# Loads, weight pieces and work units of a fused attention and feed-forward kernel in a new order, with other group sizes

## The chip, the cores and the metric

The kernel runs on one core of one Trainium2 chip. The metric is device time in microseconds (us); lower is better. Engines are called PE (TensorE, matrix multiplies), DVE (VectorE), ACT (ScalarE), POOL (GpSimd) and SP (SyncE, which here only issues DMA transfers). Each works through its own instruction list in order. A "run" is one execution; a median of several runs is quoted. A version was compared with the kernel before on the same chip, in alternating rounds.

## The reference

Linear attention with decay over 4 batches, 8 heads, 768 positions and 64 dimensions, then a feed-forward block (512 to 2048 to 512) with SiLU, all float32 at the boundary:

```python
for b in range(nb):                       # blocks of positions within a head
    intra = einsum('bhic,bhjc->bhij', qb, kb) * Dmask
    intra = einsum('bhij,bhjd->bhid', intra, vb)
    inter = einsum('bhid,bhde->bhie', qb * lam_pow, kv_state)
    out[:, :, sl] = intra + inter
    kv_state = lam_block * kv_state + einsum('bhsd,bhse->bhde', kb * rev_pow, vb)
x = out.transpose(0, 2, 1, 3).reshape(3072, 512)
h = x @ w_in
y = (h * sigmoid(h)) @ w_out
```

## The kernel before

The 3072 tokens are 24 chunks of 128, six to a batch. A chunk's attention has four pieces on PE: `t` (transposes of q and k), `d` (update of the running kv state), `s` (scores) and `o` (output, which ends as columns of `xt`). Chunks are collected into groups. For a group, 16 "up" units (`ffn1`) compute the hidden layer, 128 features each, and "down" units (`ffn2`, a quarter of the sum over features for 128 tokens) the result. The main loop mixes the up units of one group with attention pieces of the next and down units of the one before. Names in the profiles: `tp` are the transposes, `qbd` and `kt` their copies for PE, `sp` the scores and `ss` the masked scores, `kv_ps` and `kvs` the state and its copy, `op` the attention output; `hp` (later `h_ps`) and `o_ps` are the results of up and down units, `g` and `ob` their copies.

```python
GROUPS = [512, 256, 256, 512, 512, 512, 512]
wio = tile_pool(name="wio", bufs=3)      # float32 weight pieces
io  = tile_pool(name="io", bufs=7)       # q, k, v as loaded
opool = tile_pool(name="opool", bufs=3)  # results on their way out
# ... (cut)
def prep(c):
    qf, kf, vf = raw.pop(c)
    nc.gpsimd.tensor_tensor(qb, qf, <lam_fwd>, op=AL.mult)
    nc.gpsimd.tensor_tensor(kb, kf, <lam_bwd>, op=AL.mult)
    nc.scalar.activation(vb, vf, AF.Copy)        # the cast of v is issued here
# ... (cut)
def ffn2(g, mt, kos):
    # ... (cut) four matmuls into o
    if kos[-1] == KO_OUT - 1:
        nc.vector.tensor_copy(ob, o)
        nc.sync.dma_start(out=out[r0:r0 + BLK, :], in_=ob)   # same queue as the loads
# ... (cut) start: load chunks 0 to 3, then w_in; attention of chunks 0 to 3
for m in range(16):                     # up units of group 0
    ffn1(0, m)
    # ... (cut) cast_w("in", 2), cast_w("in", 3), load_w("out", 1..3) on the way
for i in range(4):
    cast_w("out", i)                    # all four casts, on DVE, ahead of chunk 4
while loads and loads[0] < n0 + 6:
    load_c(loads.pop(0))                # chunks 6 to 9 are queued at once
# ... (cut)
for g in range(1, len(GROUPS)):
    while done_c < cst[g] + nch[g]:     # attention pieces that are still missing
        next_att()                      # prepares one chunk ahead, loads one more
        next_down(g)
    npieces = 4 * (nch[g + 1] if g + 1 < len(GROUPS) else 0)
    acc = 0.0
    for m in range(16):
        ffn1(g, m)
        next_down(g)
        acc += npieces / 16.0
        while acc >= 1.0:
            next_att()
            acc -= 1.0
```

## Time and profile before

| | before |
|---|---|
| median of 3 runs | 257.65 us (256.52 to 258.14) |
| span of the profiled run | 254.6 us, mean granted PE clock 0.970 |
| PE busy in the span | 221.1 us |
| first up unit | 24.85 us |
| PE nearly idle | 40.9 to 53.2 us |

The span runs from the first to the last instruction; the device time of the same run was 256.3 us. The first excerpt is the table of stretches of the kernel before, 6 us each. After the stretch and its length it gives, for each engine, busy us and the number of instructions, then the granted clock (1.00 is full), the DMA engines' busy share, and GB/s.

```profile
...
42.00:48.00 6.00, 1.55 (x4) 0.41 (x3) 1.35 (x2) 0.00 (x0) 0.00 (x0) 0.73 1.03 387
48.00:54.00 6.00, 1.16 (x6) 0.59 (x6) 4.30 (x7) 0.00 (x0) 2.08 (x2) 0.50 1.06 235
54.00:60.00 6.00, 5.78 (x28) 3.13 (x28) 2.10 (x4) 2.15 (x5) 2.79 (x3) 0.63 1.30 224
...
```

PE works 1.55 and 1.16 of 6 us in the first two of these stretches, while the DMA engines are busy all the time, and from the second on its clock is down to 0.50 and 0.63. The second excerpt is the timeline of the kernel before: start in us, length in us, engine, line of the program, operation, output from input; in brackets the engine's idle time just before and what ended it.

```profile
...
45.17 1.23 DVE L112 CAST w_out_bf<-t 128x2048 bf16<-128x2048 f32 x1 [9.41 <-DMA t<-in_moe_w_out_dram]
46.45 1.86 PE L235 MATMUL o_ps<-w_out_bf,g 128*128 128x512 bf16 x4 [5.33 <-DVE w_out_bf L112]
...
47.88 1.23 DVE L112 CAST w_out_bf<-t 128x2048 bf16<-128x2048 f32 x1 [1.48 <-DMA t<-in_moe_w_out_dram]
...
50.67 1.23 DVE L112 CAST w_out_bf<-t 128x2048 bf16<-128x2048 f32 x1 [1.57 <-DMA t<-in_moe_w_out_dram]
...
51.81 0.41 DVE L159 COPY qbd_101<-tp 64x512 bf16<-64x512 bf16 x1
...
53.16 1.03 PE L186 MATMUL sp<-qbd_101,kt 128*128 128x256 bf16 x4 [4.84 <-DVE kt L161]
...
```

DVE waits 9.41 us for a piece of `w_out`, the second of four (the first was cast at 34.53), then for two more. Chunk 4's copies (`qbd`, at 51.81) stand behind these casts in DVE's list although their own input, the transposes, was ready at about 40. PE's score piece `sp` waits for them until 53.16. The third excerpt is the list of waits of PE over the whole kernel before: who waited for whom, us in total, how often, the longest.

```profile
...
PE sp L186 <- DVE kt L161: 6.6, 5, 4.8
PE o_ps L235 <- DVE w_out_bf L112: 5.3, 1, 5.3
PE hp L221 <- ACT xt L212: 3.4, 10, 0.4
...
```

The first two are the hole. The third is the first up units of a group, which wait for ACT to copy the last chunk's output to `xt`.

### The profile page before, as it was taken

The page shows a single profiled execution, that of the slowest core. Times are in us where ns is not written, and L with a number is a line of the kernel's source. Part 1 is how long each engine was busy: PE and PEld are TensorE (multiplying, and loading weights), DVE is VectorE, ACT ScalarE, POOL GpSimd, SP SyncE. Part 2 cuts the span into 40 slices and gives each one's busy share as a digit, 9 for nine tenths or more (in the row PEclk, how much of TensorE's full clock was granted, in tenths as well). Part 3 has the DMA queues.
Part 4 walks back from the last instruction along what each step waited for, and adds up shares of the span by engine and source line. Part 5 has one row for each costly group of instructions (what it writes and reads, how often), then busy time and mean ns, then how long its engine had stood idle before and what let it go on. Part 6 is the DMA issues. An engine that isn't in the chain of part 4 may idle for free.

```text
span 254.6 us, 3566 instructions
## 1 busy us (share of the span) xinstructions
PE 221.1 (87%) x1353; PEld 124.9 (49%) x1376; DVE 102.0 (40%) x177; ACT 112.9 (44%) x238; POOL 51.1 (20%) x57
## 2 busy tenths in 40 slices
PE   0756994269998899899998999998999999999994
PEld 0534442035567667555565555554555544444441
DVE  2678410464345457434463534453353430111221
ACT  4146774003428455736585356535535543333000
POOL 3650033063113333331242231132000000000000
PEclk9999999559999999999999999999999999999998
DMA  6999899999999766945397011101101110111122
GB/s 132 220 259 374 290 232 290 337 221 217 195 269 272 164 148 140 221 74 127 84 230 138 0 41 45 41 1 44 41 0 44 41 41 0 44 41 41 41 85 82
DMA packets 82721, 33.79 MB, mean 133 GB/s; under 512 B 75536, under 2 KB 75536, under 8 KB 82704
## 3 DMA queue, kind: packets, MB, share of 16 engines
q1 hardware_dynamic: 82560, 33.56, 56.3%
q8 instruction: 11, 0.18, 0.3%
q14 instruction: 6, 0.05, 0.1%
q10 hardware_dynamic: 144, 0.00, 0.0%
HBM read 27.27 MB, written 6.29 MB: 132 GB/s over the span
## 4 chain that ended last, share of the span: by engine, by line
PE 73%; DVE 7%; DMA 6%; ACT 5%; SPq 5%; issue 2%; POOL 1%
PE o_ps L235 32%; PE hp L221 25%; DMA t<-in_moe_w_out_dram 5%; PE sp L186 4%; PE op L206 3%; PE op L209 3%; PE tp L156 2%; DVE ss L189 2%; SPq L133 2%; ACT xt L212 2%; PE tp L154 2%; ACT xt L211 2%; PE kv_ps L173 2%; SPq L132 1%; DMA lam_sb<-in_lam_dram 1%
## 5 line engine op out<-in xcount | busy, mean ns | idle before, releaser
L221 PE MATMUL hp<-xt,w_in_bf 128*128 128x512 bf16 (+1 forms) x433 | 98.0, 347 | 6.0 <-ACT xt L212 3.4
L235 PE MATMUL o_ps<-w_out_bf,g 128*128 128x512 bf16 x376 | 96.4, 385 | 5.9 <-DVE w_out_bf L112 5.3
L224 ACT ACTIVATE g<-hp 128x512 bf16<-128x512 f32 (+1 forms) x112 | 59.7, 537 | 80.1 <-PE hp L221 78.4
L235 PEld LDWEIGHTS <-g 128*128 128x128 bf16 x384 | 38.0, 99 | 46.9 <-issue 7.1
L221 PEld LDWEIGHTS <-w_in_bf 128*128 128x128 bf16 x448 | 42.4, 98 | 37.0 <-issue 7.7
L142 POOL TENSOR_TENSOR qb<-qf,lam_fwd 128x512 bf16<-128x512 f32 x24 | 25.0, 1044 | 113.8 <-PE tp L154 76.0
L189 DVE TENSOR_TENSOR ss<-sp,mask 128x512 bf16<-128x512 f32 x48 | 31.1, 686 | 21.4 <-PE sp L186 21.2
L239 DVE COPY ob<-o_ps 128x512 f32<-128x512 f32 x24 | 16.6, 692 | 53.0 <-PE o_ps L235 53.0
L211 ACT ACTIVATE xt<-op 64x256 bf16<-64x256 f32 x48 | 18.1, 377 | 31.6 <-PE op L209 29.4
L143 POOL TENSOR_TENSOR kb<-kf,lam_bwd 128x512 bf16<-128x512 f32 x24 | 25.0, 1043 | 12.7 <-PE kv_ps L173 10.5
L206 PE MATMUL op<-ss,vb 128*128 128x256 bf16 x96 | 22.4, 284 | 0.9 <-DVE ss L189 0.6
L144 ACT ACTIVATE vb<-vf 128x512 bf16<-128x512 f32 x24 | 15.0, 625 | 9.1 <-DMA vf<-in_v_dram 9.0
L212 ACT ACTIVATE xt<-op 64x256 bf16<-64x256 f32 x48 | 18.2, 380 | 0.6
L154 PE MATMUL tp<-ident,qb 128*128 128x128 bf16 x96 | 9.7, 227 | 8.3 <-POOL qb L142 6.8
L186 PEld LDWEIGHTS <-kt 128*128 128x128 bf16 x96 | 9.1, 101 | 16.0 <-DVE kt L161 9.6
L176 DVE CAST kvs<-kv_ps 128x512 bf16<-128x512 f32 x20 | 13.7, 687 | 6.2 <-PE kv_ps L173 6.2
L154 PEld LDWEIGHTS <-qb 128*128 128x128 bf16 x96 | 7.6, 101 | 12.9 <-POOL qb L142 6.7
L206 PEld LDWEIGHTS <-vb 128*128 128x128 bf16 x96 | 9.7, 102 | 4.5 <-DVE ss L189 0.9
L159 DVE COPY qbd_99<-tp 64x512 bf16<-64x512 bf16 x8 | 3.3, 416 | 19.7 <-PE tp L156 19.7
L112 DVE CAST w_out_bf<-t 128x2048 bf16<-128x2048 f32 x4 | 4.9, 1227 | 15.4 <-DMA t<-in_moe_w_out_dram 15.4
L186 PE MATMUL sp<-qbd_101,kt 128*128 128x256 bf16 x32 | 5.6, 298 | 5.7 <-DVE kt L161 4.8
L161 DVE COPY kt<-tp 128x512 bf16<-128x512 bf16 x24 | 10.2, 425 | 0.3
(36 smaller groups left out, 98.3 us busy)
## 6 DMA issues: line engine op xcount, KB each, us to landing
qf<-in_q_dram SPq DMA_DIRECT2D x24, 256.0 KB, 4.9
kf<-in_k_dram SPq DMA_DIRECT2D x24, 256.0 KB, 5.0
vf<-in_v_dram SPq DMA_DIRECT2D x24, 256.0 KB, 5.0
out_dram<-ob SPq DMA_DIRECT2D x24, 256.0 KB, 2.0
t<-in_moe_w_in_dram SPq DMA_DIRECT2D x4, 1024.0 KB, 8.5
t<-in_moe_w_out_dram SPq DMA_DIRECT2D x4, 1024.0 KB, 9.0
lam_sb<-in_lam_dram ACTq DMA_DIRECT2D x1, 4.0 KB, 3.0
```

Source lines behind the costliest of these rows:

```text
L142: nc.gpsimd.tensor_tensor(qb, qf, lam_fwd[:, blk, :][:, :, None].to_broadcast([128, H, D]), op=AL.mult)
L143: nc.gpsimd.tensor_tensor(kb, kf, lam_bwd[:, blk, :][:, :, None].to_broadcast([128, H, D]), op=AL.mult)
L154: nc.tensor.transpose(tp[:, 0, p, :], pair_of(qb, p), ident)
L186: nc.tensor.matmul(sp[:, 2 * j:2 * j + 2, :], lhsT=kt[:, p, :], rhs=qt[:, p, :, :], start=True, stop=True)
L189: nc.vector.tensor_tensor(ss, sp, mask[:, None, :].to_broadcast([128, 4, BLK]), op=AL.mult)
L206: nc.tensor.matmul(op[:, j, :, :], lhsT=pair_of(vb, p), rhs=res[half][:, 2 * j:2 * j + 2, :], start=True, stop=(blk == 0))
L211: nc.scalar.activation(xt[g][0:64, 2 * half:2 * half + 2, csl], op[0:64, :, 0, :], AF.Copy)
L212: nc.scalar.activation(xt[g][64:128, 2 * half:2 * half + 2, csl], op[64:128, :, 1, :], AF.Copy)
L221: nc.tensor.matmul(hp[:, :n], lhsT=w_in_bf[:, ko, m * 128:(m + 1) * 128], rhs=xt[g][:, ko, :], start=(ko == 0), stop=(ko == KO_IN - 1))
L224: nc.scalar.activation(gg, hp[:, :n], AF.Silu)
L235: nc.tensor.matmul(o, lhsT=gt[g, ko][:, mt * BLK:(mt + 1) * BLK], rhs=w_out_bf[:, ko, :], start=(ko == 0), stop=(ko == KO_OUT - 1))
L239: nc.vector.tensor_copy(ob, o)
```

## The change

Its intent: PE should always have work for which the data has arrived. The first weight pieces are smaller, and the two chunks of the second group come between weight pieces; the up units of the first group start on half of its tokens; attention of chunks 4 and 5 and some down units are placed among the last up units; the `w_out` casts are spread. Groups are 512, 256, 256, 4 x 384, 512. In later stretches units, pieces and down units are sorted by fractions of the stretch. Some first-group copies go from DVE to ACT, and a table load for SiLU is brought forward. A path with DMA transposes is prepared but never taken (`NPET` is 24). Cut to its core:

```diff
-GROUPS = [512, 256, 256, 512, 512, 512, 512]
+GROUPS = [512, 256, 256, 384, 384, 384, 384, 512]
+NPET = 24
+    for i in range(NQBD):                        # for the path not taken
+        t = const.tile([128, NP, 4, D], BF16, name=f"qpad{i}")
+        nc.gpsimd.memset(t, 0.0)
+    nc.scalar.activation(warm, mask[:, 0:1], AF.Silu)
+    W_IN = [(0, 256), (256, 512), (512, 1024), (1024, 1536), (1536, 2048)]
# prep: the cast of v is put off
-        nc.scalar.activation(vb, vf, AF.Copy)
+        vraw[c] = vf                             # cast in vcast(c), later
# first group: kt and kvs on ACT, half of xt on DVE, transposes in another PSUM tag (another set of buffers for matmul results)
+        if first:
+            nc.scalar.activation(kt, tp[:, 1, :, :], AF.Copy)
# ... (cut) the start, in the order of arrival:
+    for c in range(4):
+        load_c(c)
+    for i in range(5):
+        load_w("in", i)
+        if i == 3:
+            load_c(4)
+    load_c(5)
+    load_w("out", 0)
# ... (cut) attention of chunks 0 to 3
+    ffn1(0, 0, 0), ffn1(0, 1, 0)                 # first half of the tokens
+    st_o(3)
+    ffn1(0, 0, 1), ffn1(0, 1, 1)
# ... (cut) up units 2 to 15 with chunks 4 and 5 among them
+    cast_w("out", 0)
+    st_s(5), st_d(5)
+    ffn2(0, 0, range(0, 4))
+    st_o(5)
+    ffn2(0, 1, range(0, 4))
+    load_c(6)
+    load_c(7)                                    # later loads: one for each prep
# ... (cut)
+    def stretch(*parts):                         # part: items, from, to (fractions)
+        units = []
+        for i, (items, a, z) in enumerate(parts):
+            units += [(a + (z - a) * (j + 0.5) / len(items), i, j, it) for j, it in enumerate(items)]
+        for _, _, _, (fn, *args) in sorted(units, key=lambda u: u[:3]):
+            fn(*args)
# casts: w_out casts 1 to 3; early: the down units of chunks 0 and 1 that use them
+    stretch((ups(1), 0, 1), (casts, 0.0, 0.7), (early, 0.2, 0.9), ([(next_prep,), (next_prep,)], 0.6, 0.8),
+            (downs(0, range(2, 4)), 0.9, 1.3))
+    stretch((downs(1, range(2)), 0, 1), (pieces(2), 0, 0.8))
+    for g in range(2, len(GROUPS)):
+        parts = [(ups(g), 0, 1), (pieces(g + 1), 0, 0.85)]
+        if g > 2:
+            parts.append((downs(g - 1, range(nch[g - 1])), 0, 1))
+        stretch(*parts)
```

## The prediction

> **What bounds the kernel now.** From about 66 us, the tensor engine (PE): the windows table has it busy 8.6 to 9.95 of each 10 us, and the waits list from 66 us gives it 4.1 us of waits, 3.4 of them for `xt` at group starts. Before that, arriving data. The timeline shows the first four chunks' loads issued until 14.3 us; first up-projection at 24.85; a `Silu` table load of 1.28 us at 25.3; PE dense to about 40.7. Then it stands almost still until 53.2 (busy 1.55 of 6 us in 42:48, 1.16 in 48:54), because VectorE's queue holds four `w_out` casts ahead of chunk 4's copies: one waited 9.41 us for its DMA (casts at 45.17, 47.88, 50.67). The granted clock is then 0.50 in 48:54, 0.63 in 54:60. The Trainium skill ("TensorE: Matmul & The Clock Gate", What's actually happening) says an idle window of ~3.4 us halves the clock; this trace agrees.
>
> PE's work at full clock, an estimate from trace pitches (four 512-column matmuls 0.86 us; a chunk's attention about 1.95): 82.9 + 82.9 + 24 x 1.95 = 212.6 us. The span is 254.6: 42 us are start, hole, slow clock, small waits and tail.
>
> **What the change does.** PE's operations stay. Removed: the hole and its slow clock (an estimate: 188.6 us of work remained at 53.2). `w_in` comes in smaller first pieces interleaved with chunks 4 and 5, so PE has their attention, 16 units and 2 down pieces to do while `w_out` arrives. The first up units start on half the tokens; the table load goes to the idle start; in the first group some copies move to ScalarE, and transposes take another PSUM tag, so no longer wait for `ss` (0.78 us each). Added: 16 more, shorter `Silu`; three POOL memsets for a path never taken, in its idle start: no cost.
>
> **The critical path after.** Bytes are the same; the DMA view shows chunks at about 220 GB/s, weights at 386, with 1.6 us from last byte to cast. I estimate visible: first `w_in` 21, last 34; chunk 5 37.6; `w_out` 40.3, 43, 45.7, 48.4. PE does units 0 to 11 by 34.3, waits about 2.3 us for the last `w_in` cast and chunk 4's copies queued behind it, 1 to 1.5 at chunk 5 and the first `w_out` cast, and starts group 1 at 47.2 with 27.2 us of work done. Remaining: 185.4 at full clock, 5 of waits (the down-only stretch of group 1 and the 256-token stretch carrying three chunks are tight: VectorE 3.3 of 3.6 us per chunk), 2.9 tail: span 240.5. Times run 1.7 to 3 above span: **242.5 us**, range 235 to 249. Chances: faster 0.96, same 0.03, slower 0.01. Nearly all the gain is before 66 us; the 384-token groups bring 2 us or less.
>
> **What would show it.** Right: no PE wait above 3 us after 25; clock 1.00 from 15 us; first up unit at 21.5 to 22.5, group 1 at 46 to 49; PE busy 9.7 of 10 from 60; `xt` waits below 1.5 us. Wrong: half clock after 40; `hp` waiting over 3 us for `w_in` casts; many `sp` or `op` waits for VectorE in stretches with two or three chunks.
>
> **What would make it wrong.** VectorE, waiting in order for a weight piece, could hold PE until the clock halves (3 to 6 us slower); chunks 8 to 11 could be late in the short 256-token stretch; better DMA overlap could bring 235.

## The result and the profile after

The changed kernel took 243.66 us (median of 4 runs, 243.06 to 244.62), against 257.65 before. The ratio is 0.9466 with a 95% interval of 0.9418 to 0.9515. Ratios here are the mean time of one kernel's fast runs over that of the other's of the same rounds, so they are not quite the ratio of the medians. The profiled run's span is 241.4 us.

| | before | after |
|---|---|---|
| median | 257.65 us | 243.66 us |
| span, granted clock of the profiled run | 254.6, 0.970 | 241.4, 0.997 |
| first up unit | 24.85 us | 24.12 us |
| up unit 2 of group 0 starts | about 27.3 us | 28.05 us |
| first up unit of group 1 | 64.0 us | 47.90 us |

First the same stretches of the changed kernel.

```profile
...
42.00:48.00 6.00, 4.96 (x35) 2.85 (x34) 5.16 (x8) 3.54 (x9) 0.00 (x0) 1.00 1.03 378
48.00:54.00 6.00, 5.83 (x43) 3.99 (x41) 1.94 (x2) 3.25 (x9) 2.32 (x2) 1.00 0.94 207
54.00:60.00 6.00, 6.00 (x42) 4.02 (x41) 1.25 (x2) 2.23 (x7) 3.37 (x4) 1.00 1.16 217
...
```

The hole and the half clock are gone. The DMA engines were nearly as busy as before (378, 207 and 217 GB/s against 387, 235 and 224). Next the timeline of the changed kernel around the arrival of `w_out`.

```profile
...
44.03 1.22 DVE L145 CAST w_out_bf<-w_tmp 128x2048 bf16<-128x2048 f32 x1
...
45.30 1.02 PE L308 MATMUL o_ps<-w_out_bf,g 128*128 128x512 bf16 x4 [0.52 <-DVE w_out_bf L145]
...
46.36 2.35 DVE L145 CAST w_out_bf<-w_tmp 128x2048 bf16<-128x2048 f32 x2
...
47.90 2.40 PE L293 MATMUL h_ps<-xt,w_in_bf 128*128 128x256 bf16 x16
...
50.58 1.23 DVE L145 CAST w_out_bf<-w_tmp 128x2048 bf16<-128x2048 f32 x1 [1.87 <-DMA w_tmp<-in_moe_w_out_dram]
...
51.39 1.32 POOL L174 TENSOR_TENSOR qb<-qf,lam_fwd 128x512 bf16<-128x512 f32 x1 [13.93 <-DMA qf<-in_q_dram]
...
```

The four casts of `w_out` start between 44.0 and 50.6; before, one started at 34.5 and the others between 45.2 and 50.7. The last piece thus comes no earlier, but now PE has attention, up units and early down units in between, and waits 0.52 us for one cast. The last line shows POOL starting on chunk 6's q as it lands, at 51.39, where the kernel before did at 51.82: by then as many bytes have arrived. The list of waits of PE of the changed kernel:

```profile
...
PE sp L248 <- ACT kt L217: 3.2, 3, 1.6
...
PE o_ps L308 <- DVE w_out_bf L145: 0.5, 1, 0.5
PE h_ps L293 <- ACT xt L279: 0.4, 1, 0.4
...
```

What did not improve is the start. The timeline of the changed kernel shows chunk 3 on its way to the first up unit:

```profile
...
16.45 0.42 PE L268 MATMUL op<-ss,vb 128*128 128x256 bf16 x1
...
16.66 0.42 PE L271 MATMUL op<-qbd_101,kvs 128*128 128x256 bf16 x1
...
20.27 0.27 PE L268 MATMUL op<-ss,vb 128*128 128x256 bf16 x1
...
20.37 0.27 PE L271 MATMUL op<-qbd_103,kvs 128*128 128x256 bf16 x1
...
21.43 0.60 ACT L217 ACTIVATE kt<-tp 128x512 bf16<-128x512 bf16 x1 [0.81 <-DVE qbd_99 L215]
...
22.08 0.61 PE L248 MATMUL sp<-qbd_99,kt 128*128 128x256 bf16 x4 [0.78 <-ACT kt L217]
...
22.70 0.63 ACT L143 ACTIVATE w_in_bf<-w_tmp 128x512 bf16<-128x512 f32 x1
...
23.24 0.62 ACT L191 ACTIVATE vb<-vf 128x512 bf16<-128x512 f32 x1
23.90 0.38 PE L232 MATMUL kv_ps<-vb,kb 128*128 128x128 bf16 x4 [1.21 <-ACT vb L191]
...
24.12 1.04 PE L293 MATMUL h_ps<-xt,w_in_bf 128*128 128x256 bf16 x8
...
```

The last six lines are a chain through ACT, which now does the `kt` copy, a weight cast and the v cast one after the other; the first up unit stands behind the kv matmuls at 24.12. Unit 2, which follows all of units 0 and 1, starts at 28.05, later than the 27.3 of the kernel before. So the rearranged first units bring nothing that these traces show; the gain is after 40 us.

The first four lines show the clock by the spacing of matmuls of equal size: 0.21 us apart until 18 us, 0.10 to 0.11 after. That agrees with the Trainium skill ("TensorE: Matmul & The Clock Gate", What's actually happening), which calls the half clock the default until activity releases it. It would explain why four transposes took 0.61 us at first and 0.39 later. When the full clock comes differs from run to run: in the kernel before, matmuls of 256 columns already stand 0.11 us apart at 16.24, and in the experiment without memsets below, whose start is otherwise that of the changed kernel, the score piece at 13.94 takes 0.61 us, where the one at 13.91 here takes 1.03. There unit 2 starts at 27.45, so about 0.6 us of the later start is the clock of this one run.

The changed kernel has two sorts of fast runs: spans of 241.4 us at a mean clock of 0.997 or 0.998, and of 242.5 to 242.9 at 0.993. No trace of the second sort was kept for this kernel. One was for the experiment with 512-token groups and pieces over the whole stretch, which has the same start: its clock is 0.57 in 24 to 28 us, and the first up unit's eight matmuls take 1.83 us in place of 1.04. Differences near 1 us between versions have to be read with that in mind.

### The profile page after: what moved, and what is told of

Same layout as the page of the kernel before. It is cut to its first block, busy times and chain, and to the rows that moved or that the text cites. A ratio compares the mean times of both kernels' runs of the same rounds, so it can differ in the third digit from the quotient of the medians.

```text
span 241.4 us, 3766 instructions
## 1 busy us (share of the span) xinstructions
PE 220.5 (91%) x1448; PEld 131.4 (54%) x1448; DVE 102.1 (42%) x178; ACT 118.3 (49%) x257; POOL 55.2 (23%) x60
## 4 chain that ended last, share of the span: by engine, by line
PE 83%; DVE 7%; ACT 5%; issue 2%; DMA 1%; POOL 1%; ACTq 0%; DVEq 0%
PE o_ps L308 33%; PE h_ps L293 32%; PE op L268 4%; PE op L271 3%; PE sp L248 3%; PE tp L211 2%; PE tp L209 2%; PE kv_ps L232 2%; DVE ss L251 2%; DMA lam_sb<-in_lam_dram 1%; ACT xt L279 1%; DVE kt L219 1%; ACT xt L278 1%; ACT kt L217 1%; ACT vb L191 1%
## 5 line engine op out<-in xcount | busy, mean ns | idle before, releaser
L293 PE MATMUL h_ps<-xt,w_in_bf 128*128 128x384 bf16 (+2 forms) x520 | 99.5, 323 | 1.6 <-ACT g L297 0.8
L297 ACT ACTIVATE g<-h_ps 128x384 bf16<-128x384 f32 (+2 forms) x128 | 62.3, 491 | 76.1 <-PE h_ps L293 75.1
L308 PE MATMUL o_ps<-w_out_bf,g 128*128 128x512 bf16 x384 | 94.9, 379 | 0.5 <-DVE w_out_bf L145 0.5
L293 PEld LDWEIGHTS <-w_in_bf 128*128 128x128 bf16 x520 | 50.0, 98 | 35.1 <-issue 2.8
L278 ACT ACTIVATE xt<-op 64x256 bf16<-64x256 f32 x44 | 16.6, 377 | 18.9 <-PE op L271 9.9
L279 ACT ACTIVATE xt<-op 64x256 bf16<-64x256 f32 x44 | 16.7, 380 | 0.5
L238 DVE CAST kvs<-kv_ps 128x512 bf16<-128x512 f32 x16 | 11.0, 685 | 1.9 <-PE kv_ps L232 1.9
L211 PE MATMUL tp<-ident,kb 128*128 128x128 bf16 x96 | 10.0, 230 | 0.4 <-POOL kb L183 0.4
L271 PEld LDWEIGHTS <-kvs 128*128 128x128 bf16 x80 | 8.0, 100 | 3.9 <-issue 1.3
L232 PE MATMUL kv_ps<-vb,kb 128*128 128x128 bf16 x80 | 8.2, 228 | 1.5 <-ACT vb L191 1.5
L232 PEld LDWEIGHTS <-kb 128*128 128x128 bf16 x80 | 6.5, 102 | 4.5 <-issue 2.2
```

Of the source, the lines that this page charges most:

```text
L232: nc.tensor.matmul(kv[:, p, :], lhsT=pair_of(kb, p), rhs=pair_of(vb, p), start=(blk == 0 and p == 0), stop=True, skip_group_check=True)
L278: nc.scalar.activation(xt[g][0:64, ps, csl], op[0:64, :, 0, :], AF.Copy)
L279: nc.scalar.activation(xt[g][64:128, ps, csl], op[64:128, :, 1, :], AF.Copy)
L293: nc.tensor.matmul(hp[:, a:z], lhsT=w_in_bf[:, ko, m * 128:(m + 1) * 128], rhs=xt[g][:, ko, a:z], start=(ko == 0 and a == 0), stop=(ko == ...
L297: nc.scalar.activation(gg, hp[:, :n], AF.Silu)
L308: nc.tensor.matmul(o, lhsT=gt[g, ko][:, mt * BLK:(mt + 1) * BLK], rhs=w_out_bf[:, ko, :], start=(ko == 0), stop=(ko == KO_OUT - 1))
```

## The experiments

Twelve kernels ran, all with correct results, with five further rounds each. The kernel before had medians of 257.06, 255.88, 255.65 and 256.03 us in the four submissions; versions are best compared within one submission. All came out of one question: which part of the change makes the gain?

### Submission 1 (before: 257.06 us)

**Only the `w_out` casts moved, in the kernel before.** This is the reading of the prediction taken alone: fill the hole by putting three casts and their down units behind the attention of chunks 4 and 5. Chunk 6 and 7's pieces come after group 1's up units.

```diff
-    for i in range(4):
+    for i in range(1):
         cast_w("out", i)
# ... (cut)
+    late = [1, 2, 3]                # cast just ahead of the first down unit that needs it
+        if g == 0:
+            order = [(mt, kk) for kk in range(4) for mt in range(2)] + order[8:]
# ... (cut) next_down:
+            if late and downs[0][2][0] == 4 * late[0]:
+                cast_w("out", late.pop(0))
# ... (cut) main loop:
             next_att()
-            next_down(g)
+            if g > 1:
+                next_down(g)
-        npieces = 4 * (nch[g + 1] if g + 1 < len(GROUPS) else 0)
+        npieces = 4 * (nch[g + 1] if 1 < g < len(GROUPS) - 1 else 0)
```

> The kernel before, with one thing changed: three of the four w_out casts, and the down pieces that use them, come after the attention of chunks 4 and 5, and group 2's attention after group 1's up units. No small weight pieces, no new load order, no engine moves, 512-token groups. Theory A (the gain is the filled hole at 41 to 53 us and its half clock): PE dense from 46 to 48 us, clock 1.00 throughout, 246 to 249 us. Rival B (arrival order, small first weight pieces and half units make the gain): no better than 254.

Measured: 259.04 us (257.99 to 260.36), ratio 1.0084. Theory A failed in this form, and the number alone would have favoured the rival. The timeline of this experiment tells why:

```profile
...
49.45 3.48 DVE L112 CAST w_out_bf<-t 128x2048 bf16<-128x2048 f32 x3
...
55.01 0.63 ACT L144 ACTIVATE vb<-vf 128x512 bf16<-128x512 f32 x1 [8.85 <-DMA vf<-in_v_dram]
55.66 0.38 ACT L211 ACTIVATE xt<-op 64x256 bf16<-64x256 f32 x1
...
56.48 0.58 PE L221 MATMUL hp<-xt,w_in_bf 128*128 128x256 bf16 x2 [5.60 <-ACT xt L212]
...
```

The casts no longer stand in the way, and chunk 5's output was computed by 51. But `prep(6)` had put chunk 6's v cast into ACT's list ahead of chunk 5's `xt` copies; it waited 8.85 us for its DMA, and the up units of group 1 for `xt`, 5.60 us, until 56.48. A second wait of the same kind had been hidden behind the first: in the kernel before that v cast ran only at 58.44, when its data had landed.

**The groups of before, in the changed kernel.**

```diff
-GROUPS = [512, 256, 256, 384, 384, 384, 384, 512]
+GROUPS = [512, 256, 256, 512, 512, 512, 512]
```

> The changed kernel with the groups of before (512-token groups in place of 384). Theory A: the start is the same to 66 us; 0 to 2 us slower, so 243.5 to 245.5. Rival C (the smaller groups carry a good part of the gain): 248 or more.

Measured: 248.58 us (247.90 to 249.79), ratio 0.9679: 4.9 us slower than the changed kernel's 243.66, more than the prediction allowed. The rival's number was met. At equal clock (0.997) the spans are 246.2 and 241.4. The timeline of this experiment shows one of the places:

```profile
...
142.85 0.60 PE L248 MATMUL sp<-qbd,kt 128*128 128x256 bf16 x4
...
143.27 1.29 DVE L251 TENSOR_TENSOR ss<-sp,mask 128x512 bf16<-128x512 f32 x2 [2.23 <-PE sp L248]
...
144.02 0.27 PE L268 MATMUL op<-ss,vb 128*128 128x256 bf16 x1 [0.56 <-DVE ss L251]
...
```

The output piece follows its score piece with nothing between, so PE waits for DVE's masking in full. In the order of instructions this happens four times (0 us of PE work between `s` and `o`), and never in the changed kernel, where that distance is at least 0.43 us of work. With 16 pieces in 0.85 of a stretch and 16 up and 16 down units in all of it, two pieces sometimes fall between the same two units. The four waits add up to 2.3 us. Part of the rest shows in the 256-token stretch: from 66 to 108 us, PE is busy 37.9 us here and 40.0 in the changed kernel (one of the four waits lies in it). Four chunks' attention rather than three is pressed there between the 16 small up units; that this is the reason was not tested by itself.

**The first group's engine moves undone, in the changed kernel.** `kt`, `kvs` and weight casts on DVE, all `xt` copies on ACT, transposes in the `att` buffers.

```diff
-        if first:
-            nc.scalar.activation(kt, tp[:, 1, :, :], AF.Copy)
-        else:
-            nc.vector.tensor_copy(kt, tp[:, 1, :, :])
+        nc.vector.tensor_copy(kt, tp[:, 1, :, :])
# likewise kvs, xt, the first two weight casts and the PSUM tag
```

> The changed kernel with the first group's engine moves undone: kt and kvs copies back on VectorE, all xt copies and no weight cast on ScalarE, transposes back in the att buffers. Theory A: the up units of the first group wait for the last w_in piece (cast at 34.3) in any case, so group 1 starts within 0.7 us of 47.9 and the time is within 1 us of the changed kernel, even if the first up unit shifts by 1 to 2 us. Rival D (the moves shorten the start): 1.5 to 4 us slower.

Measured: 242.53 us (241.68 to 242.74), ratio 0.9429: 1.1 us faster than the changed kernel's two medians (243.66, and 243.65 for the next experiment, which equals it). Part of that is the clock: five of those ten runs are of the 0.993 sort and none of the six here. Among the runs at 0.997 or more the spans are 239.9 to 241.0 here and 241.0 to 241.6 there, 0.8 us apart in the mean. The rival is out: the moves do not shorten the start, they lengthen it a little. But my reason was wrong too. The first up unit starts at 23.19 in place of 24.12, unit 2 at 27.38 in place of 28.05, and the shift is still there at the end; the last `w_in` piece did not absorb it. A reason why moving `kt` to ACT brings nothing is in the Trainium skill ("PSUM — Partial Sum Buffer", PSUM bank collisions raise a hardware error): two engines may not touch one bank and quadrant at once, reads included, so the program has to put one after the other. This trace agrees: in the changed kernel DVE's copies of that bank end at 9.20 and ACT's `kt` copy, which waited for them, starts at 9.30 and takes 0.60 us; on DVE it starts at 9.23 and takes 0.42. No run put the two in different banks.

**Attention pieces to the end of the stretch, in the changed kernel.**

```diff
-        parts = [(ups(g), 0, 1), (pieces(g + 1), 0, 0.85)]
+        parts = [(ups(g), 0, 1), (pieces(g + 1), 0, 1)]
```

> The changed kernel with the attention pieces of the next group spread over the whole stretch (fraction 1 in place of 0.85). Theory A: the waits of the first up unit of each group for xt come back, about 0.4 to 0.5 us for each of six groups, so 2 to 3 us slower (245.5 to 247). Rival E (placement does not matter once PE is dense): within 0.7 us.

Measured: 243.65 us (242.71 to 244.66), ratio 0.9484: no difference. The waits for `xt` do come back, but only 1.1 us of them after 60 us (four waits), and waits for `kt` fall from 0.9 to 0.8 us. So the fraction of 0.85 as such is worth nothing that these runs can show.

### Submission 2 (before: 255.88 us)

**All v casts out of the preparation, on top of the first experiment.** The v cast goes from `prep` to the head of `st_d`.

```diff
-        nc.scalar.activation(vb, vf, AF.Copy)
+        vraw[c] = vf
# ... (cut)
+    def vcast(c):
+        if c in vraw:
+            nc.scalar.activation(natb[c][2], vraw.pop(c), AF.Copy)
# st_d, first lines:
+        qb, kb, vb = natb[c]
+        vcast(c)
```

> The first experiment showed a second block behind the first: ScalarE's cast of v for chunk 6, issued ahead of chunk 5's xt copies, waited for its DMA until 55.0, and the up units of group 1 for xt until 56.5. This kernel is the first experiment with the v casts moved out of the preparation to the kv piece, as the change does. Theory A2 (the hole is two in-order waits, one on VectorE and one on ScalarE, and both have to go): group 1 starts at 50 to 52 in place of 56.5, no wait over 3 us after 45, 251 to 254 us. Rival: another block appears and it stays at 257 or more.

Measured: 264.69 us, ratio 1.0323. Slower still. One of six runs took 478.64 us, and that was the profiled one. Slow runs are not compared, so this profile explains nothing; that the kv matmuls of every chunk then wait for ACT was argued from the order, not shown (the slow profile lists six such waits, 5.7 us in all).

**512-token groups with the pieces over the whole stretch, in the changed kernel.** The two edits of submission 1 together.

```diff
-GROUPS = [512, 256, 256, 384, 384, 384, 384, 512]
+GROUPS = [512, 256, 256, 512, 512, 512, 512]
-        parts = [(ups(g), 0, 1), (pieces(g + 1), 0, 0.85)]
+        parts = [(ups(g), 0, 1), (pieces(g + 1), 0, 1)]
```

> 512-token groups as in the second experiment, with the pieces over the whole stretch, so that no score piece is followed at once by its output piece (four times in that experiment, with 0.64 us of stall each). Theory F (of the 4.9 us that the 384-token groups bring, about 2 come from fractions that fall together in the 512-token stretches, the rest from four chunks in the 256-token stretch): 246 to 247.2 us. Rival (the size itself matters): 248 or more.

Measured: 245.93 us (244.72 to 246.74), ratio 0.9592, against 243.6 for the next kernel, which equals the changed one. So of the 4.9 us, this edit takes back 2.6; at a clock of 0.997 or more the spans are 243.0 to 243.6, against 246.2. The coinciding fractions are gone with it: PE's waits for `ss` after 60 us, 2.3 us in four before, are no longer listed. The remaining 2.3 us belong to the 512-token groups with the stretch that feeds them; this experiment does not divide them further.

**The last `w_in` and first `w_out` piece loaded ahead of chunks 4 and 5, in the changed kernel.**

```diff
     for i in range(5):
         load_w("in", i)
-        if i == 3:
-            load_c(4)
-    load_c(5)
     load_w("out", 0)
+    load_c(4)
+    load_c(5)
```

> The changed kernel with the last w_in piece and the first w_out piece loaded ahead of chunks 4 and 5. Same bytes, so the arrival of the last thing needed is the same. Theory A: the last w_in piece is cast at about 30.5 in place of 34.3, chunk 4 comes about 4 us later than before and PE waits for it instead; group 1 starts within 1 us of 47.9, and the time is within 1 us of the changed kernel. Rival B (the arrival order matters): 2 us or more slower.

Measured: 243.60 us (243.43 to 244.69), ratio 0.9517: the same. The last `w_in` cast starts at 30.46 in place of 34.34, POOL's work on chunk 4's q at 34.17 in place of 27.89, and PE waits for neither. The exact arrival order of these four pieces does not matter; between 28 and 48 us the changed kernel has slack in both.

**A 256-token first group.** Chunks 0 and 1, `w_in`, chunks 2 and 3, `w_out`; groups 256, 256, 4 x 384, 2 x 512; engine moves and memsets out.

```diff
-GROUPS = [512, 256, 256, 384, 384, 384, 384, 512]
+GROUPS = [256, 256, 384, 384, 384, 384, 512, 512]
+    load_c(0), load_c(1)
+    for i in range(4):
+        load_w("in", i)
+    load_c(2), load_c(3)
# ... (cut) attention of chunks 0 and 1; up units 0 to 11 with three w_in casts
+    prep(2)
+    cast_w("in", 3)
# ... (cut) loads of the last w_out piece and of chunks 4 to 6
+    ffn1(0, 12), ffn1(0, 13)
+    st_t(2)
+    ffn1(0, 14), ffn1(0, 15)
+    prep(3)
+    st_s(2), st_d(2)
+    st_t(3), st_o(2), st_s(3), st_d(3), st_o(3)
# stretch of group 1, with all early down units of group 0:
+    stretch((ups(1), 0, 0.45), (casts, 0.0, 0.5), (early, 0.12, 0.6), (downs(1, range(2)), 0.6, 1), (pieces(2), 0.5, 0.95))
# ... (cut) engine moves and memsets taken out as in their own experiments
```

> A new start: first group of 256 tokens, so two chunks, w_in, two chunks, w_out, then the rest; first-group engine moves and unused memsets left out; groups 256, 256, 4 x 384, 2 x 512. Theory G (up to 48 us PE is limited by what has arrived, and weights bring more work per byte than chunks): estimate from 220 and 386 GB/s: last w_in cast at 24.5, last w_out at 42.4, PE dense from 26 to 33 on, 15 to 17 us of idle up to 42 in place of 20.7 up to 47.9; 237 to 240.5 us. Rival (start is bound by the chain of attention, not by arrival): 242 or more.

Measured: 241.68 us (240.94 to 242.51), ratio 0.9428 (0.9385 to 0.9472): the lowest median, 1.9 us below the changed kernel's equal. But it also leaves out the engine moves, and the changed kernel without these had a ratio of 0.9429 in submission 1. By the ratio, then, the smaller first group adds nothing to that; by the distance to the changed kernel's equal (1.9 us here, 1.1 there) it would add 0.8 us. The runs do not settle it; this version beats both kernels, and the removal of the engine moves can account for at least a good part. It is less than theory G expected. The up units of group 0 start at 17.27 in place of 24.12, but most of that is given back, as this excerpt of its timeline shows:

```profile
...
17.27 8.05 PE L283 MATMUL h_ps<-xt,w_in_bf 128*128 128x256 bf16 x56 [0.26 <-DVE w_in_bf L141]
...
29.62 0.40 PE L205 MATMUL tp<-ident,qb 128*128 128x128 bf16 x4 [1.10 <-POOL qb L170]
30.62 0.40 PE L207 MATMUL tp<-ident,kb 128*128 128x128 bf16 x4 [0.60 <-POOL kb L179]
...
35.43 0.38 PE L283 MATMUL h_ps<-xt,w_in_bf 128*128 128x256 bf16 x2 [0.42 <-ACT xt L269]
...
```

Chunk 3 now arrives late (PE waits for POOL's preparation of it at 29.62 and 30.62), its attention is a chain of waits with no other work beside it, and group 1's up units begin at 35.43.

### Submission 3 (before: 255.65 us)

**Only chunk 6's v cast moved, on top of the first experiment.**

```diff
-        nc.scalar.activation(vb, vf, AF.Copy)
+        if c == 6:
+            vraw[c] = vf                # cast at the head of st_d(6)
+        else:
+            nc.scalar.activation(vb, vf, AF.Copy)
```

> The kernel of the first experiment with only chunk 6's v cast moved behind chunk 5's xt copies; all other v casts stay in the preparation (moving all of them to the kv piece let the kv matmuls of every chunk wait for ScalarE, and cost 5 us more). Theory A2 (two in-order waits make the hole: VectorE for w_out, ScalarE for v of chunk 6): group 1 starts at 50 to 52 in place of 56.5, 251 to 254.5 us, no PE wait over 3 us after 20. Rival: 257 or more.

Measured: 259.18 us (256.86 to 259.84), ratio 1.0107. Group 1 starts at 51.27, as theory A2 said, and PE is dense to 75. The time did not fall, and once more the timeline names the next wait:

```profile
...
72.59 1.09 SPq L133 DMA_DIRECT2D vf<-in_v_dram  x1
...
73.78 6.48 SPq L248 DMA_DIRECT2D out_dram<-ob  x4
...
79.20 0.69 DVE L246 COPY ob<-o_ps 128x512 f32<-128x512 f32 x1 [10.87 <-DMA out_dram<-ob]
79.81 0.41 DVE L164 COPY qbd<-tp 64x512 bf16<-64x512 bf16 x1
...
81.15 1.04 PE L193 MATMUL sp<-qbd,kt 128*128 128x256 bf16 x4 [5.96 <-DVE kt L166]
...
```

`SPq` is the queue from which SP issues transfers. The stores of the first results stand in it behind the loads of chunks 6 to 12, which fill it until 73.68. There are three `ob` buffers, so DVE's fourth `ob` copy waits 10.87 us for the first store to land, chunk 6's copies stand behind it in DVE's list, and PE waits 5.96 us. The clock is at half from 79.7 to 86.5 after it.

**The changed kernel without the unused memsets.**

```diff
-    for i in range(NQBD):
-        t = const.tile([128, NP, 4, D], BF16, name=f"qpad{i}")
-        nc.gpsimd.memset(t, 0.0)
-        qpad.append(t)
```

> The changed kernel without the three unused memsets on POOL. The profile of the changed kernel shows VectorE's 128x6 cast at 2.46 taking 2.30 us in place of 0.11 while they run. Expected: that cast is back at about 0.11 us, lam_fwd still starts at 5.2 to 5.4 because ScalarE's table load ends then, and the time is the changed kernel's within 0.7 us.

Measured: 244.25 us (242.50 to 244.98), ratio 0.9543: no difference. DVE's small cast goes back from 2.30 us (first excerpt, changed kernel) to 0.11 (second, this experiment):

```profile
...
2.00 0.95 POOL L86 MEMSET qpad_105<- 128x1024 bf16 x1
...
2.46 2.30 DVE L92 CAST iota_f<-iota_i 128x6 f32<-128x6 int32 x1
...
5.27 0.24 ACT L102 ACTIVATE lam_fwd<-lam_exp 128x48 f32<-128x48 f32 x1
...
```

```profile
...
2.46 0.11 DVE L88 CAST iota_f<-iota_i 128x6 f32<-128x6 int32 x1
...
5.30 0.24 ACT L98 ACTIVATE lam_fwd<-lam_exp 128x48 f32<-128x48 f32 x1
...
```

`lam_fwd` starts at 5.27 and 5.30: ACT's table load ended then in both (3.98 and 4.01, each with 1.28 us). The Trainium skill ("SBUF — State Buffer", Terms) says that DVE and POOL share a port pair under an exclusive lock. The trace agrees that DVE was held while POOL worked, for as long as all three memsets lasted, and no longer without them; that it was by this lock, no run shows.

**Chunks 2 and 3 among the `w_in` pieces, on top of the small first group**, with their attention among the up units and each `w_in` cast split between DVE and ACT.

```diff
-    for i in range(4):
-        load_w("in", i)
-    load_c(2), load_c(3)
+    load_w("in", 0), load_c(2), load_w("in", 1), load_c(3), load_w("in", 2), load_w("in", 3)
# cast_w: every w_in piece, half on each engine
+        if which == "in":
+            nc.vector.tensor_copy(dst[:, 0:2, :], t[:, 0:2, :])
+            nc.scalar.activation(dst[:, 2:4, :], t[:, 2:4, :], AF.Copy)
# ... (cut) t, s, d, o of chunks 2 and 3 between up units 3 and 11
```

> As the small first group, with chunks 2 and 3 loaded between the w_in pieces and their attention between the up units, and each w_in cast split between VectorE and ScalarE. In the small-first-group run chunks 2 and 3 came after w_in, and group 1's up units waited until 35.4 us with 14.7 us of PE work done. Theory G: up units dense from 26 to 28 us, group 1 starts at 31 to 33, and the time falls by 2.5 to 4 us to 237.5 to 239.5. Rival (arrival is not what limits the start, or small gains are eaten later): 241 or more.

Measured: 244.17 us (243.28 to 245.26), ratio 0.9539. Worse than the version it was meant to improve; a run of the small first group in the same submission was not made, but the difference of 2.5 us is more than the medians of equal kernels vary here (243.60 to 244.25). Its timeline shows up units waiting 1.25 us at 18.69 and 0.84 us at 35.88 for the ACT half of a weight cast, which stands behind other ACT work: the same mistake. The list of waits also has 6.3 us of `sp` for DVE's `kt`, in seven waits (3.6 us in the small first group), and this profile is of a run at a clock of 0.986; how the 2.5 us divide is not shown.

### Submission 4 (before: 256.03 us)

**The loads paced, on top of the kernel with chunk 6's v cast moved.**

```diff
-    while loads and loads[0] < n0 + 6:
+    while loads and loads[0] < n0 + 2:
```

> The profile of the previous kernel of this series shows the first hole filled (group 1 at 51.3 us, PE dense to 75) and a third in-order wait behind it: the first output stores stand on the DMA-issuing queue behind the loads of chunks 6 to 12, so VectorE's fourth ob copy waits 10.9 us for a buffer, chunk 6's copies behind it, PE 5.96 us, and the clock halves for 6.8 us. This kernel only paces the loads as the change does (chunks 6, 7, 8 ahead of the first stores in place of 6 to 12). Theory A3 (three in-order waits on three queues, one behind the other, make the hole; each must go): no PE wait over 2 us after 20, no half clock after 40, 249.5 to 252 us. Rival (the hole only moves again, or the late loads make a new wait): 255 or more.

Measured: 250.64 us (249.63 to 251.67), ratio 0.9802 (0.9750 to 0.9855): inside the interval expected of theory A3. The interval of the ratio reaches over 0.98, so whether the gain is over 2% is not settled; that this kernel is faster than the earlier steps (1.0107 and 1.0084) is. The list of waits of PE from 46 to 90 us in this kernel:

```profile
...
PE sp L193 <- DVE kt L166: 1.9, 3, 1.4
PE hp L228 <- ACT xt L219: 0.7, 2, 0.4
PE op L213 <- DVE ss L196: 0.6, 1, 0.6
```

No wait is over 1.4 us, and the last PE instruction starts at 243.9 us in place of 254.0 in the kernel of the step before. One of the six runs still had a mean clock of 0.973; the others are at 0.999 or 1.000.

## Why the prediction was right, point by point

- **The time.** 242.5 us was predicted with 235 to 249, 243.66 measured. The mechanism, filling the hole at 41 to 53 us, is shown: three moves in the kernel before that do only this bring 5.4 us, and the first or the first two of them bring nothing. It is shown for this part of the gain, not for all of it (see the sum below).
- **The cause of the hole was named incompletely.** The prediction gave one in-order wait, DVE's `w_out` casts. The runs show three on three queues: those casts on DVE, chunk 6's v cast on ACT, and the stores behind seven chunks' loads on SP. The kernel before showed only the first, as PE was late enough for the others to be over. The change undoes all three (spread casts, `vcast`, one load for each preparation). That the prediction still came out right rests on its reading the new order, not on having found the others; that the change removed them too was luck for the prediction. The three moves were tried in one order only: the paced loads alone, or without the v cast, were not run, so it is shown that the first two do not suffice, not that each is needed.
- **Group 1 at 47.2.** Measured 47.90, within the 46 to 49 given. Two terms in it were off and cancelled. The first up unit was put at 21.5 to 22.5 and came at 24.12, because the moves to ACT, counted as help, form a chain there (23.19 without them), and because the full clock came late in this run (23.53 in the run without memsets, where it came early). The wait of 2.3 us for the last `w_in` piece did not happen: PE came to it late, and the largest wait between 28 and 48 us was 0.54 us.
- **384-token groups: 2 us or less.** This term failed in size. They bring 4.9 us, of which 2.6 come from fractions that no longer coincide. So "nearly all the gain is before 66 us" did not hold either: about a third is after. The prediction looked at busy shares of DVE in the tight stretches, not at which piece follows which. Its time was not hurt, as the sum for the changed kernel does not use this term.
- **Waits of 5 us after group 1.** From 47.90 to the last PE work at 237.6 are 189.7 us, for an estimate of 185.4 us of work; 4.3 us in place of 5. The listed waits after 60 us are 1.5 us, so part of the 4.3 is work that the estimate put too low.
- **`xt` waits below 1.5 us.** They fell from 3.4 to 0.4 us, as said. The experiment that brought 1.1 us of them back did not change the time, so this sign was right and not worth what it seemed.
- **The other signs.** No listed PE wait after 25 us is over 0.6 us, where 3 was the bound. "PE busy 9.7 of 10 from 60" holds from 100 us on; from 70 to 100 it is 9.2 to 9.5, in the stretches that the prediction called tight. "Clock 1.00 from 15 us" holds in the clock column, but by the spacing of matmuls the full clock came at 18 us.
- **The memsets cost nothing.** Right for the time; they did hold DVE for 2.2 us where it had slack.
- **Chunks at about 220 GB/s, weights at 386.** Both patterns held in the changed kernel (221 and 232 GB/s in 6 to 18 us, 378 in 42 to 48). The Trainium skill ("DMA: Bandwidth & Descriptors", Why small descriptors are slow (HBM only)) explains slower small transfers by a fixed cost per packet; q, k and v rows are 64 floats, 256 bytes. No run here changed that size, so the cause is taken from the page, not shown.

Of the 14 us, then, about 5.4 come from the three moves and about 4.9 from the groups. The other 3 to 4 us lie between the kernel of submission 4 and the changed kernel with the old groups (250.64 and 248.58), and in the spread of the kernel before (255.65 to 257.65). They were not divided further: placing chunks 4 and 5 among up units is a likely part, as the submission 4 kernel starts group 1 at 49.63, 1.7 us later, with 1.7 us less PE work done (two down pieces of 0.86 us). That is argued, not shown.

## What to carry to other kernels

When an engine idles because something ahead of it in a list waits for a transfer, look at all in-order lists, the DMA-issuing one included, for the next entry that would wait if this one were gone; filling a hole may do nothing at all until the last of them is moved, as here. The Trainium skill ("PSUM — Partial Sum Buffer", Engine vs sequencer instructions) says that the queues of ScalarE, VectorE and GpSimd are strictly in order, and the trace agrees: behind the waits of 9.41, 8.85 and 10.87 us here, work whose own input was ready stood still. And when work is interleaved by fractions, print the resulting order and check that no dependent pair has become neighbours: that was worth about 2.6 us here, more than the fraction of 0.85 itself.

## What the Trainium skill lacked or had wrong

- "SBUF — State Buffer", SBUF: two separate sides: it says that the lock is held for the whole instruction. Here a 128x6 DVE cast of 0.11 us took 2.30 us, through the rest of one POOL memset and two more behind it; the page does not say that back-to-back instructions can keep the other engine out.
- "TensorE: Matmul & The Clock Gate": it gives the default clock as half, which agrees, and warns that clock events in a trace can be unreliable, but not that a profile's clock column may show 1.00 until the first clock record. In the changed kernel the column shows 1.00 from the start, while matmuls of 256 columns stand 0.21 us apart until 18 us, and 0.11 after; the first clock record in the packed trace is at 18.2 us.
- The same page calls the warm-up run-variable and small, and the runs agree: spans of 241.4 and of 242.5 to 242.9 us for the changed kernel, 0.5% apart. Its table puts the return to the half clock after an idle window. In the trace of the 512-token groups with pieces over the whole stretch the clock falls to half at 24.3 us and PE was not idle before: it was busy 1.4 of the 3.4 us from 20.9 to 24.3. The page's part on short idle gaps (PSUM queue cycling) tells of something like it, without a busy share.
- No page that I found describes one run of six at 478.64 us on a single core, with four 512-column matmuls every 1.89 us in place of 0.86; the TensorE page only tells of a clock stuck at a quarter for over 50 us. The clock column is at 1.00 throughout, but this trace has no clock record at all. DVE's casts take 1.23 us as in other runs, so it is PE that is slow: an estimate of 212.6 us of PE work times 1.89 / 0.86 is 467 us of the span of 476.8. Why PE stayed slow is open.
- "DMA: Bandwidth & Descriptors", Specifications: it gives about 358 GB/s as the limit of one core's share of memory, without a condition. With one core running, weight pieces moved at 387 GB/s in the kernel before (42 to 48 us). The page's own Measured part, with more than that for a core whose neighbour is idle, fits better.
- "PSUM — Partial Sum Buffer" and "DMA: Bandwidth & Descriptors": neither warns that a store issued on the queue of the loads waits for them to be issued, and holds the compute engine that fills its buffer: 10.87 us here. The DMA page says only that descriptors of a ring are consumed in order.
